# Output weights put into head order on the chip, attention outputs multiplied with them directly, and finer loads near the end: a decode attention kernel on Trainium2

## Chip, cores and metric

The kernel runs on one core of one Trainium2 chip. The metric is the device time of one execution in microseconds (us): before the change a median of 1379.54 us over three runs, from 1379.39 to 1380.29. The profile read below is of one execution with a span of 1378.5 us and a mean granted TensorE clock of 0.905.

## What is computed

Two attention blocks for a single decode step. Both have 4 batch rows, 32 query heads of size 128, a model width of 512 and bf16 data. Block A has 8 key/value heads and looks at the last 2048 positions only; block B has 32 key/value heads and looks at all 8192 positions. The two results stand side by side in the output.

```
def _B_ref(x, k_cache, v_cache, wq, wo):
    B, Sq, D = x.shape                      # 4, 1, 512
    H, Dh = 32, 128
    q = (x @ wq).reshape(B, Sq, H, Dh).transpose(0, 2, 1, 3)
    scores = einsum("bhqd,bhkd->bhqk", q, k_cache) * (Dh ** -0.5)
    p = softmax(scores)
    o = einsum("bhqk,bhkd->bhqd", p, v_cache)
    return o.transpose(0, 2, 1, 3).reshape(B, Sq, H * Dh) @ wo
# A: the same with 8 key/value heads, each used by 4 query heads,
#    and only the last 2048 of 8192 positions
```

B's keys and values are 268 MB each, out of 587.51 MB that the whole kernel moves.

## The kernel before

**Chunks.** Block A is 8 chunks (one per key/value head, all four batch rows). Block B is 32 chunks: one chunk is four heads of one batch row. They are taken group by group: a group is four heads (`hq`, 0 to 7), and inside a group the four batch rows follow one another. A chunk of B is 256 tiles of 128 x 128 keys and as many of values, 8.39 MB each.

**The work on one chunk of B** (`whole_B`, L771) is written out in program order for every engine:

1. 32 steps `g`, each of 8 tiles: TensorE transposes the 8 key tiles into a PSUM bank of `tr` (`emit_T`, three banks), VectorE or ScalarE copies them to `kt` in SBUF, and two steps later TensorE multiplies them with the query `qq` into the scores `sc` (`emit_S`).
2. Statistics: VectorE takes the row maxima (`stats_rowmax`), TensorE turns them (`stats_gmax`), VectorE reduces, TensorE spreads the result (`stats_bc`), VectorE writes `negb`.
3. ScalarE takes the exponentials in eight instructions, two halves of four heads (`exp_B`), VectorE sums them (`sums_B`).
4. 256 matmuls of probabilities with value tiles into `po` (`emit_pv`); at step 20 of 32 the sums are turned into reciprocals (`norm_sum`).
5. `norm_out` scales `po` into `oz`, a 128 x 16 tile that holds four heads of this batch row and zeros elsewhere.

**Output projection.** The weights of a group, `wos`, are loaded as they lie in HBM: partition p holds rows 4p to 4p+3 of the group's 512 rows. So a head's 128 rows lie on 32 partitions, four rows on each, while `oz` has a head's 128 values on 128 partitions. Before the change the outputs are brought into the order of the weights: `emit_sel` (L679) multiplies `oz` with four 0/1 matrices `sel4` into `ms`, and four small copies put the result into `zB`. Then `emit_fin` (L700) adds to `fin` with 8 matmuls, four for each half of the 512 output columns. For chunk c-1 these two stand inside the keys of chunk c: `emit_sel` after step g = 1, `emit_fin` after g = 4. For the last chunk they stand after everything else, and `emit_out` copies `fin` to SBUF and starts the stores.

**Loads and their order.** All loads of keys, values and weights are issued in one fixed order by one queue, SyncE's, and a load that waits holds up all those behind it. Keys have one buffer of a chunk's size, values have one. The keys of chunk c+1 come in two pieces of 128 tiles; a piece may start when the chunk c has transposed the quarters of the buffer that it overwrites. The values of chunk c+1 are one piece and may start when all 256 value matmuls of chunk c are done. Exceptions at the end: the last chunk's keys come in pieces of `LASTK`, its values in `LASTV`, the values of the last but one in `NEXTV` = (128, 64, 64) tiles. GpSimd waits for each piece and counts it into the semaphores `r_k` and `r_v`, which TensorE waits on before certain steps (`QK`, `QV`).

For the first chunk of each group but the first, the queue holds: two key pieces, then `wos` of the new group, then the values. The reload of `wos` waits for `emit_fin` of the last chunk of the old group (L344), which is in step 4 of the chunk just begun.

Of the kernel before, what the change touches and what calls it, by code (L numbers as in the profile page):

```python
# [6 lines left out]
ACTF = mybir.ActivationFunctionType  # L7
# [160 lines left out]
def bass_concat_heads__sliding_block_cached__mha_block_cached__decode_kernel(  # L168
# [39 lines left out]
    NTA, NTB = chunks[0]["NT"], chunks[-1]["NT"]  # L208
    NONE = NC
    chunks.append(dict(chunks[NCA]))  # L210
    assert sum(LASTV) == sum(LASTK) == sum(NEXTV) == NTB and NTA * 16 == 1024 and NTB * 4 == 1024

    sch = _Sched()
    with ExitStack() as es:
        block = es.enter_context(nc.Block())

        def sb(name, shape, dt):
            return es.enter_context(nc.sbuf_tensor(name, shape, dt))
# [47 lines left out]
        semnames += [f + str(i) for f, x in (("d_lk", LASTK), ("d_lv", LASTV), ("d_nv", NEXTV)) for i in range(len(x))]  # L266
# [31 lines left out]
        for r in range(4):  # L298
            sch.add("pool", lambda e, r=r: e.affine_select(
                out=sel4[:, r, :], in_=onesb[:, :], pattern=[[0, 4], [-4, 32]], compare_op=ALU.is_equal,  # L300
                fill=0.0, base=-r, channel_multiplier=1), waits=["c_onesb"], key="c_sel" if r == 3 else None)


        half_of = {}
# [34 lines left out]
        def dma_wos(hq):  # L339


            src = B_wo[4 * hq * P:4 * (hq + 1) * P, :].rearrange("(p r) n -> p (r n)", r=4)
            sch.add_dma("sp", lambda e: e.dma_start(wos[:, :, :].rearrange("p r n -> p (r n)"), src), "d_wos",
                        waits=[("fin", NCA + 4 * hq - 1)] if hq else [], key=("wos", hq))  # L344

        def dma_A(kind, c):
            ch = chunks[c]
# [6 lines left out]
        def dma_B(kind, c):  # L354


            ch = chunks[c]
            T, at, steps = (B_k, KB, QK) if kind == "k" else (B_v, VB, QV)
            src = T[ch["b"], 4 * ch["hq"]:4 * ch["hq"] + 4].rearrange("u (pp j) d -> (u pp) (j d)", pp=P // 4)
            dst = flat(at, 4)  # L360
            if kind == "k":
                pieces, fam = (LASTK, "d_lk") if c == NC - 1 else ((NTB // 2,) * 2, "d_bk")
            else:
                pieces, fam = (LASTV, "d_lv") if c == NC - 1 else (NEXTV, "d_nv") if c == NC - 2 else ((NTB,), "d_bv")
            j0, unit = 0, NTB // 4
            for i, n in enumerate(pieces):
                waits = []
                for u in range(j0 // unit, (j0 + n - 1) // unit + 1):
                    waits += held[at + u]
                x = slice(j0 * P, (j0 + n) * P)  # L370
                sch.add_dma("sp", lambda e, x=x: e.dma_start(dst[:, x], src[:, x]), fam + str(i), waits=waits, key=(kind, c, i))
                j0 += n
                sch.relay("pool", sems, "r_" + kind, n // TG, [(kind, c, i)] + ([("wos", ch["hq"])] if i == 0 and (kind == "v" if c > NCA else kind == "k") else []))
# [292 lines left out]
        def norm_out(c):  # L666
            if c < NCA:
                m = c % NSM
                o, i0, i1 = oT[:, m, :], po[:, m * 16:m * 16 + 16], rinv[:, m, :]
                waits = [("rinv", c), ("pv", c)] + ([("sm", c - 2)] if c >= 2 else [])  # L670
            else:

                o, i0 = oz[:, :].rearrange("p (b u) -> p b u", b=NB), bcast(po[:, 0:4], [[0, NB], [1, 4]])
                i1 = rz[:, :].rearrange("p (b u) -> p b u", b=NB)
                waits = [("rz", c), ("pv", c), ("sm", prev(c))]
            sch.add("dve", lambda e: e.tensor_tensor(out=o, in0=i0, in1=i1, op=ALU.mult), waits=waits, key=("oT", c))  # L676
            po_read[:] = [("oT", c)]

        def emit_sel(c):  # L679

            ab = 0 if c < NCA else 1
            if ab == 0:
                x, z, free = oT[:, c % NSM, :], zA[:, c % 2, :], [("fin", c - 2)] if c >= 2 else []
            else:
                x, z, free = oz[:, :], zB[:, :], [("fin", prev(c))] if c != NONE else []
            for r in range(4):
                pe_mm(ms[:, Z0 + r * 16:Z0 + (r + 1) * 16], sel4[:, r, :], x,
                      waits=([("oT", c)] if c != NONE else []) + (["c_oz", "c_sel"] if ab else []) + ms_read if r == 0 else [], key=("sm", c) if r == 3 else None)
            for h in range(4):
                pp = slice(h * P // 4, (h + 1) * P // 4)  # L690
                src, dst = ms[pp, Z0:Z0 + 64].rearrange("p (r b h) -> p h r b", r=4, b=NB)[:, h], z[pp, :].rearrange("p (r b) -> p r b", r=4)
                if c == NC - 1 and h % 2:
                    sch.add("act", lambda e, src=src, dst=dst: e.activation(dst, src, ACTF.Copy),
                            waits=[("sm", c)] + free if h == 1 else [], key=("z2", c) if h == 3 else None)
                else:
                    sch.add("dve", lambda e, src=src, dst=dst: e.tensor_copy(dst, src),  # L696
                            waits=[("sm", c)] + free if h == 0 else [], key=("z", c) if h == (2 if c == NC - 1 else 3) else None)
            ms_read[:] = [("z", c)] + ([("z2", c)] if c == NC - 1 else [])

        def emit_fin(c):  # L700
            ab = 0 if c < NCA else 1
            if ab == 1:
                ops = [(zB[:, r * NB:(r + 1) * NB], wos[:, r, :]) for r in range(4)]
                waits = [("z", c)] + ([("z2", c)] if c == NC - 1 else [])
# [12 lines left out]
            if c == lastc:  # L717
                emit_out(c)
# [52 lines left out]
        def whole_B(c):  # L771


            ch, p = chunks[c], prev(c)
            sch.mark()
            emit_qb(c)
            for g in range(ch["NG"]):
                emit_T(ch["s"] + g)
                if g == 1:
                    emit_sel(p)  # L780
                if g == 4:
                    emit_fin(p)
                if g >= SLAG:
                    emit_S(ch["s"] + g - SLAG)
                if g == ch["NG"] // 2 + SLAG + 1:
                    stats_rowmax(c, 0)
            for g in range(SLAG):
                emit_S(ch["s_last"] + 1 - SLAG + g)
            stats_rowmax(c, 1)
            stats_gmax(c)  # L790
            stats_bc(c)
            exp_B(c)
            sums_B(c)
            for g in range(ch["NG"]):
                emit_pv(c, g)
                if g == 20:
                    norm_sum(c)
            norm_out(c)
# [86 lines left out]
```

## Time and profile before

| | before |
|---|---|
| device time, median of 3 | 1379.54 us (1379.39 to 1380.29) |
| span of the profiled execution | 1378.5 us |
| bytes moved, mean rate | 587.51 MB, 426 GB/s |
| TensorE matmul busy | 1161.0 us (84%) |
| VectorE busy | 682.3 us (49%) |
| ScalarE busy | 514.0 us (37%) |
| chain of waits: DMA | 54% |
| chain of waits: TensorE | 40% |
| largest link: landing of B's values | 47% |

The busy shares of engines are averages over stages in which different things end last, so they only say where to look. The strip of 40 slices shows at what time an engine or the DMA was busy. The chain of waits follows the last instruction back to what released it, step by step; an entry such as "DMA kv<-in_B_v_cache_dram" is the time from the issue of a load to its landing, in which other loads ahead of it in the queue are included.

### The profile page before, as it was taken

What the parts mean: (1) busy time and instruction counts of PE and PEld (TensorE: products, weight loads), DVE (VectorE), ACT (ScalarE), POOL (GpSimd) and SP (SyncE); (2) the same over time, 40 slices, a digit from 0 to 9 for tenths busy, and PEclk for the clock granted to TensorE, in tenths of its full rate; (3) what the DMA queues carried; (4) which work ended last, traced back from release to release, by engine and by line L of the source; (5) the groups of instructions that cost most, each with busy time, mean ns of one, the idle gap of its engine ahead of it and who ended that gap; (6) DMA issues with size and microseconds to landing.
All of it is one profiled execution on the core that took longest, in us unless ns stands there. A gap on an engine that the chain in (4) does not pass through costs nothing.

```text
span 1378.5 us, 60077 instructions
## 1 busy us (share of the span) xinstructions
PE 1161.0 (84%) x27036; PEld 1117.0 (81%) x27037; DVE 682.3 (49%) x1337; ACT 514.0 (37%) x651; POOL 6.8 (0%) x24
## 2 busy tenths in 40 slices
PE   4898788889888788898888788898888888988887
PEld 4786688889887788888888788898878788987887
DVE  1675355555444445554444455554444455544444
ACT  1553234433333334433333344333333344333333
POOL 1000000000000000000000000000000000000000
PEclk9998899999999989999999898998999999989999
DMA  9999999999999999999999999999999999999996
GB/s 401 425 426 442 415 425 432 433 422 443 430 434 434 426 433 433 434 438 435 430 430 424 434 435 431 434 440 434 432 428 430 431 434 433 441 430 432 428 421 260
DMA packets 20220, 587.51 MB, mean 426 GB/s; under 512 B 2260, under 2 KB 2280, under 8 KB 4712
## 3 DMA queue, kind: packets, MB, share of 16 engines
q1 hardware_dynamic: 20168, 587.21, 99.1%
q8 instruction: 15, 0.25, 0.1%
q14 instruction: 5, 0.04, 0.0%
q10 hardware_dynamic: 32, 0.01, 0.0%
HBM read 587.21 MB, written 0.01 MB: 426 GB/s over the span
## 4 chain that ended last, share of the span: by engine, by line
DMA 54%; PE 40%; DVE 3%; issue 2%; ACT 1%; SPq 0%; DVEq 0%; POOLq 0%; ACTq 0%
DMA kv<-in_B_v_cache_dram 47%; PE po L407 22%; PE tr L405 10%; DMA kv<-in_B_k_cache_dram 6%; PE sc L407 6%; DMA kv<-in_B_wq_dram 2%; PE ms L407 1%; ACT pbb L587 1%; PE fin L407 1%; DVE kt L472 1%; DVE sA L525 1%; DVE rh L541 0%; PE ms L405 0%; DVE rm L537 0%; DVE sA L523 0%
## 5 line engine op out<-in xcount | busy, mean ns | idle before, releaser
L405 PE MATMUL tr<-identb,kv 128*128 128x128 bf16 x8704 | 660.6, 220 | 9.7 <-POOLq L71 4.9
L470 ACT ACTIVATE kt<-tr 128x1024 bf16<-128x1024 bf16 x352 | 359.6, 1024 | 720.2 <-PE tr L405 720.0
L472 DVE COPY kt<-tr 128x1024 bf16<-128x1024 bf16 x736 | 499.2, 690 | 209.1 <-PE tr L405 205.4
L405 PEld LDWEIGHTS tr<-identb,kv 128*128 128x128 bf16 x8704 | 505.9, 98 | 15.2 <-issue 5.7
L407 PE MATMUL po<-pbb,kv 128*128 128x64 bf16 x8192 | 311.9, 208 | 118.2 <-POOLq L71 97.9
L407 PE MATMUL sc<-qq,kt 128*128 128x64 bf16 x8192 | 397.9, 191 | 15.3 <-DVE kt L472 11.2
L407 PEld LDWEIGHTS po<-pbb,kv 128*128 128x128 bf16 x8192 | 308.4, 109 | 120.4 <-issue 63.2
L407 PEld LDWEIGHTS sc<-qq,kt 128*128 128x128 bf16 x8192 | 328.1, 98 | 27.8 <-DVE kt L472 14.3
L587 ACT ACTIVATE pbb<-sc,negb 32x128 bf16<-32x128 f32 x256 | 137.3, 536 | 124.2 <-DVE negb L570 121.0
L592 DVE TENSOR_REDUCE rsb<-pbb 128x4 f32<-128x1024 bf16 x32 | 39.0, 1220 | 142.7 <-ACT pbb L587 142.7
L654 DVE RECIPROCAL rinv<-ms 128x4 f32<-128x4 f32 (+1 forms) x40 | 7.8, 196 | 162.1 <-PE ms L407 162.1
L541 DVE TENSOR_REDUCE rh<-sc 128x4 f32<-128x512 f32 x64 | 43.9, 686 | 14.3 <-PE sc L407 14.3
L405 PE MATMUL ms<-identf,rm 128*4 128x128 f32 x40 | 11.1, 276 | 35.2 <-DVE rm L544 31.4
L676 DVE TENSOR_TENSOR oz<-po,rz 128x16 bf16<-128x16 f32 x32 | 5.6, 175 | 67.4 <-PE po L407 67.4
L405 PEld LDWEIGHTS ms<-identf,rm 128*4 128x4 f32 x40 | 3.2, 81 | 39.3 <-DVE rm L544 34.3
L407 PE MATMUL sc<-qb,kt 128*128 128x64 bf16 (+3 forms) x512 | 26.0, 196 | 0.5 <-issue 0.2
L407 PEld LDWEIGHTS ms<-gm,ind 4*128 4x128 f32 x64 | 10.5, 203 | 18.1 <-DVE gm L556 18.1
L407 PE MATMUL po<-pba,kv 128*128 128x64 bf16 x512 | 20.5, 199 | 3.7 <-issue 2.3
L407 PEld LDWEIGHTS sc<-qb,kt 128*128 128x128 bf16 x512 | 21.8, 101 | 2.0 <-issue 1.4
L407 PE MATMUL ms<-gm,ind 4*128 4x4 f32 x64 | 13.3, 276 | 11.9 <-DVE gm L556 11.9
L696 DVE CAST zB<-ms 32x16 bf16<-32x16 f32 x130 | 21.8, 168 | 1.7 <-PE ms L407 0.4
L407 PEld LDWEIGHTS po<-pba,kv 128*128 128x128 bf16 x512 | 17.9, 102 | 5.7 <-ACT pba L609 4.2
(61 smaller groups left out, 207.1 us busy)
## 6 DMA issues: line engine op xcount, KB each, us to landing
kv<-in_B_k_cache_dram SPq DMA_DIRECT2D x62, 4096.0 KB, 26.7
kv<-in_A_k_cache_dram SPq DMA_DIRECT2D x8, 2048.0 KB, 12.4
kv<-in_A_v_cache_dram SPq DMA_DIRECT2D x8, 2048.0 KB, 13.8
kv<-in_B_v_cache_dram SPq DMA_DIRECT2D x2, 4096.0 KB, 19.3
kv<-in_B_v_cache_dram SPq DMA_DIRECT2D x3, 2048.0 KB, 24.5
kv<-in_B_k_cache_dram SPq DMA_DIRECT2D x3, 2048.0 KB, 26.5
kv<-in_A_wq_dram SPq DMA_DIRECT2D x1, 4096.0 KB, 12.2
kv<-in_B_wq_dram SPq DMA_DIRECT2D x1, 4096.0 KB, 27.1
```

The lines of the kernel that those rows point to most:

```text
L405: sch.add("pe", lambda e: e.transpose(o, l, r), waits, key)
L407: sch.add("pe", lambda e: e.matmul(o, l, r, start=start, stop=stop), waits, key)
L470: sch.add("act", lambda e: e.activation(dst, src, ACTF.Copy), waits=waits, key=("ev", s))
L472: sch.add("dve", lambda e: e.tensor_copy(dst, src), waits=waits, key=("ev", s))
L525: emit = lambda e, src=src, b=b: e.scalar_tensor_tensor(out=t, in0=src, scalar=mk[:, b:b + 1], in1=t, op0=ALU.mult, op1=ALU.add)
L541: sch.add("dve", lambda e: e.tensor_reduce(out=rh[:, half, :], in_=src, axis=AX.X, op=ALU.max), waits=[("S", ch["s"] + (half + 1) * ch["NG ...
L587: sch.add("act", lambda e, src=src, dst=dst, pp=pp, u=u: e.activation(dst, src, ACTF.Exp, bias=negb[pp, 0, u:u + 1], scale=scale), waits=[ ...
L592: sch.add("dve", lambda e: e.tensor_reduce(out=rst[1][:, :], in_=probs_of(c).rearrange("p j u -> p u j"), axis=AX.X, op=ALU.add), waits=[( ...
L654: sch.add("dve", lambda e: e.reciprocal(out=ri, in_=ms[:, L0:L0 + n]), waits=[("L", c)], key=("rinv", c))
L676: sch.add("dve", lambda e: e.tensor_tensor(out=o, in0=i0, in1=i1, op=ALU.mult), waits=waits, key=("oT", c))
L696: sch.add("dve", lambda e, src=src, dst=dst: e.tensor_copy(dst, src), waits=[("sm", c)] + free if h == 0 else [], key=("z", c) if h == (2 ...
```

## The change

The weights are brought into head order instead of the outputs. In each chunk of B, after the last scores, 16 matmuls (`reorder`) multiply the 32 partitions of `wos` that hold one head u with 0/1 matrices `back`, four per head, and leave that head's 128 x 512 weights in a bank of `tr`. Four copies by VectorE (`take_wol`) put them into `wol`, which lies in a part of `kv` that block B doesn't use. `emit_fin` then takes `oz` as it is, together with `wol`; `emit_sel`, its copies and `zB` go away for block B, and `emit_fin` moves from step 4 to step 1 of the following chunk. Three heads are reordered ahead of the turn of the maxima, the fourth after it, since there are three banks.

Since `wos` is now read by `reorder` and not by `emit_fin`, its reload waits for the last reordering of the old group, and it has been put ahead of the new group's keys in the queue. The purpose is a shorter end after the last values and a values load that doesn't wait for the projection. Besides, the keys of the last chunk but one come in three pieces (`NEXTK`), and the values of the last chunk but two in the three pieces of `NEXTV`.

```
+NEXTK = (64, 64, 128)
...
-        zB = sb("zB", [P, 16], BF16)
+        back = sb("back", [P, 4, P], BF16)
+        wol = kv[:, 8, 0:4 * DO].rearrange("p (u n) -> p u n", u=4)
...
             sch.add_dma("sp", lambda e: e.dma_start(wos[:, :, :].rearrange("p r n -> p (r n)"), src), "d_wos",
-                        waits=[("fin", NCA + 4 * hq - 1)] if hq else [], key=("wos", hq))
+                        waits=[("reord", NCA + 4 * hq - 1)] if hq else [], key=("wos", hq))
...
-                pieces, fam = (LASTK, "d_lk") if c == NC - 1 else ((NTB // 2,) * 2, "d_bk")
+                pieces, fam = (LASTK, "d_lk") if c == NC - 1 else (NEXTK, "d_nk") if c == NC - 2 else ((NTB // 2,) * 2, "d_bk")
             else:
-                pieces, fam = (LASTV, "d_lv") if c == NC - 1 else (NEXTV, "d_nv") if c == NC - 2 else ((NTB,), "d_bv")
+                pieces, fam = (LASTV, "d_lv") if c == NC - 1 else (NEXTV, "d_nv") if c in (NC - 2, NC - 3) else ((NTB,), "d_bv")
...
         for c in range(NCA, NC):
-            if c == NCA:
-                dma_wos(0)
+            if (c - NCA) % NB == 0:
+                dma_wos((c - NCA) // NB)
             dma_B("k", c)
-            if c > NCA and (c - NCA) % NB == 0:
-                dma_wos((c - NCA) // NB)
             dma_B("v", c)
...
+        def reorder(c, u, bank):
+            pp = slice(u * P // 4, (u + 1) * P // 4)
+            o = tr[:, bank, :].bitcast(F32)
+            for r in range(4):
+                pe_mm(o, back[pp, r, :], wos[pp, r, :], start=r == 0, stop=r == 3,
+                      waits=([("wol", c, 0)] if u == 3 else [("c_back", 3)]) if r == 0 else [], ...)
+
+        def take_wol(c, u, bank):
+            o = tr[:, bank, :].bitcast(F32)
+            sch.add("dve", lambda e: e.tensor_copy(wol[:, u, :], o), ...)
...
-                ops = [(zB[:, r * NB:(r + 1) * NB], wos[:, r, :]) for r in range(4)]
+                ov = oz[:, :].rearrange("p (b u) -> p b u", b=NB)
+                ops = [(ov[:, :, u], wol[:, u, :]) for u in range(4)]
...
                 emit_T(ch["s"] + g)
                 if g == 1:
-                    emit_sel(p)
-                if g == 4:
                     emit_fin(p)
...
             stats_rowmax(c, 1)
+            reorder(c, 0, 0)
+            reorder(c, 1, 1)
+            reorder(c, 2, 2)
             stats_gmax(c)
             stats_bc(c)
             exp_B(c)
+            for u in range(3):
+                take_wol(c, u, u)
+            reorder(c, 3, 0)
+            take_wol(c, 3, 0)
             sums_B(c)
...
         sch.mark()
-        emit_sel(NC - 1)
         emit_fin(NC - 1)
```

More of the change, by code (lines that the diff above doesn't have):

```diff
@@ L210, in bass_concat_heads__sliding_block_cached__mha_block_cached__decode_kernel @@
     chunks.append(dict(chunks[NCA]))
-    assert sum(LASTV) == sum(LASTK) == sum(NEXTV) == NTB and NTA * 16 == 1024 and NTB * 4 == 1024
+    assert sum(LASTV) == sum(LASTK) == sum(NEXTK) == sum(NEXTV) == NTB and NTA * 16 == 1024 and NTB * 4 == 1024
     sch = _Sched()
@@ L265, in bass_concat_heads__sliding_block_cached__mha_block_cached__decode_kernel @@
         semnames += ["d_h%d" % i for i in range(NH)] + ["d_bk0", "d_bk1", "d_bv0"]
-        semnames += [f + str(i) for f, x in (("d_lk", LASTK), ("d_lv", LASTV), ("d_nv", NEXTV)) for i in range(len(x))]
+        semnames += [f + str(i) for f, x in (("d_lk", LASTK), ("d_nk", NEXTK), ("d_lv", LASTV), ("d_nv", NEXTV)) for i in range(len(x))]
         semnames += ["d_wo%d" % i for i in range(NWO)] + ["d_wos"]
@@ L301, in bass_concat_heads__sliding_block_cached__mha_block_cached__decode_kernel @@
                 fill=0.0, base=-r, channel_multiplier=1), waits=["c_onesb"], key="c_sel" if r == 3 else None)
+        sch.add("pool", lambda e: e.memset(back[:, :, :], 0.0), waits=["c_sel"], key="c_back0")
+        for u in range(4):
+            sch.add("pool", lambda e, u=u: e.affine_select(
+                out=back[:, :, :], in_=back[:, :, :], pattern=[[1, 4], [-1, P]], compare_op=ALU.not_equal,
+                fill=1.0, base=-P * u, channel_multiplier=4), waits=["c_back0" if u == 0 else ("c_back", u - 1)], key=("c_back", u))
         half_of = {}
@@ L372, in dma_B @@
                 j0 += n
-                sch.relay("pool", sems, "r_" + kind, n // TG, [(kind, c, i)] + ([("wos", ch["hq"])] if i == 0 and (kind == "v" if c > NCA else kind == "k") else []))
+                sch.relay("pool", sems, "r_" + kind, n // TG, [(kind, c, i)] + ([("wos", ch["hq"])] if i == 0 and kind == "k" and ch["b"] == 0 else []))
             for g, end in zip(steps, steps[1:] + (NTB // TG,)):
@@ L674, in norm_out @@
                 i1 = rz[:, :].rearrange("p (b u) -> p b u", b=NB)
-                waits = [("rz", c), ("pv", c), ("sm", prev(c))]
+                waits = [("rz", c), ("pv", c), ("fin", prev(c))]
             sch.add("dve", lambda e: e.tensor_tensor(out=o, in0=i0, in1=i1, op=ALU.mult), waits=waits, key=("oT", c))
@@ L679, in emit_sel @@
         def emit_sel(c):
[L681 to L685, printed above, removed]
+            z = zA[:, c % 2, :]
             for r in range(4):
-                pe_mm(ms[:, Z0 + r * 16:Z0 + (r + 1) * 16], sel4[:, r, :], x,
-                      waits=([("oT", c)] if c != NONE else []) + (["c_oz", "c_sel"] if ab else []) + ms_read if r == 0 else [], key=("sm", c) if r == 3 else None)
+                pe_mm(ms[:, Z0 + r * 16:Z0 + (r + 1) * 16], sel4[:, r, :], oT[:, c % NSM, :],
+                      waits=[("oT", c)] + ms_read if r == 0 else [], key=("sm", c) if r == 3 else None)
             for h in range(4):
@@ L691, in emit_sel @@
                 src, dst = ms[pp, Z0:Z0 + 64].rearrange("p (r b h) -> p h r b", r=4, b=NB)[:, h], z[pp, :].rearrange("p (r b) -> p r b", r=4)
[L692 to L698, printed above, removed]
+                sch.add("dve", lambda e, src=src, dst=dst: e.tensor_copy(dst, src),
+                        waits=[("sm", c)] + ([("fin", c - 2)] if c >= 2 else []) if h == 0 else [], key=("z", c) if h == 3 else None)
+            ms_read[:] = [("z", c)]
+        def reorder(c, u, bank):
[3 more added lines that the diff above has]
+                pe_mm(o, back[pp, r, :], wos[pp, r, :], start=r == 0, stop=r == 3,
+                      waits=([("wol", c, 0)] if u == 3 else [("c_back", 3)]) if r == 0 else [], key=("reord", c) if u == r == 3 else ("reord", c, u) if r == 3 else None)
+        def take_wol(c, u, bank):
+            o = tr[:, bank, :].bitcast(F32)
+            sch.add("dve", lambda e: e.tensor_copy(wol[:, u, :], o),
+                    waits=[("reord", c) if u == 3 else ("reord", c, u)] + [("fin", prev(c))], key=("wol", c, u))
         def emit_fin(c):
@@ L702, in emit_fin @@
             if ab == 1:
-                ops = [(zB[:, r * NB:(r + 1) * NB], wos[:, r, :]) for r in range(4)]
-                waits = [("z", c)] + ([("z2", c)] if c == NC - 1 else [])
+                ov = oz[:, :].rearrange("p (b u) -> p b u", b=NB)
+                ops = [(ov[:, :, u], wol[:, u, :]) for u in range(4)]
+                waits = ["c_oz"] + ([("oT", c), ("wol", c, 3)] if c != NONE else [])
             else:
```

## The prediction

> **What bounds the kernel now.** I read the strip of 40 slices, then the chain of waits, then the issue queue, then single chunks in order of time.
>
> ```profile
> DMA  9999999999999999999999999999999999999996
> GB/s 401 425 426 442 415 425 432 433 422 443 430 434 434 426 433 433 434 438 435 430 430 424 434 435 431 434 440 434 432 428 430 431 434 433 441 430 432 428 421 260
> DMA kv<-in_B_v_cache_dram 47%; PE po L407 22%; PE tr L405 10%; DMA kv<-in_B_k_cache_dram 6%; PE sc L407 6%; DMA kv<-in_B_wq_dram 2%; PE ms L407 1%; ACT pbb L587 1%; PE fin L407 1%; DVE kt L472 1%; DVE sA L525 1%; DVE rh L541 0%; PE ms L405 0%; DVE rm L537 0%; DVE sA L523 0%
> ```
>
> The transfers run at full rate from start to near the end. Values land at 740.34 and, eight chunks later, at 1053.18 (issue plus time to landing in the chain): 39.1 us a chunk for 16.78 MB and a quarter of a weight load (0.13 MB), 432 GB/s. So half a chunk's keys cost 9.7 us, its values 19.4. Up to some 1366 us any gap in the transfers is lost one for one, and TensorE time is free while TensorE waits for values. The last slice is different: no transfers, only work.
>
> The issue queue, columns start, duration, what:
>
> ```profile
> 711.96 0.33 SPq L371 DMA_DIRECT2D kv<-in_B_v_cache_dram  x1
> 723.26 11.15 SPq L371 DMA_DIRECT2D kv<-in_B_k_cache_dram  x2
> 753.90 0.33 SPq L343 DMA_DIRECT2D wos<-in_B_wo_dram  x1
> 754.27 0.44 SPq L371 DMA_DIRECT2D kv<-in_B_v_cache_dram  x1
> ```
>
> This is the last chunk of a group. Its values are issued at 711.96; the two key pieces of the next chunk at 723.26 and about 734 lie behind them, so when the values have landed the engines have 19.4 us of keys to go on with. The reload of wos comes 3.7 us after the value buffer is free (750.2), and by then about 6 us of keys are still queued (9.7 + 9.7 us from 740.3 lasts to 760): that wait costs nothing now.
>
> TensorE in the same chunk (duration, engine, op, in brackets the idle time before it):
>
> ```profile
> 734.84 0.35 PE L407 MATMUL sc<-qq,kt 128*128 128x32 bf16 x8 [0.30 <-DVE kt L472]
> 736.17 0.27 PE L405 MATMUL ms<-identf,rm 128*4 128x128 f32 x1 [0.98 <-DVE rm L544]
> 736.82 0.38 PE L407 MATMUL ms<-gm,ind 4*128 4x4 f32 x2 [0.37 <-DVE gm L556]
> 740.52 2.72 PE L407 MATMUL po<-pbb,kv 128*128 128x64 bf16 x48 [3.32 <-POOLq L71]
> ```
>
> The scores end at 735.19, the values land 5.15 us later. At the other group ends the same distance is 4.9 to 5.8 us. In the last chunk nothing is waited for but work:
>
> ```profile
> 1360.00:1364.00 4.00, 0.65 (x3) 0.37 (x3) 1.29 (x4) 1.74 (x4) 0.00 (x0) 0.79 0.97 396
> 1364.00:1368.00 4.00, 3.55 (x67) 3.55 (x68) 1.22 (x1) 2.55 (x5) 0.00 (x0) 0.50 0.31 116
> 1368.00:1372.00 4.00, 4.00 (x118) 4.00 (x116) 0.13 (x1) 0.00 (x0) 0.00 (x0) 0.86 0.00 0
> 1372.00:1376.00 4.00, 3.19 (x95) 2.75 (x91) 0.74 (x5) 0.35 (x2) 0.00 (x0) 1.00 0.00 0
> ```
>
> Columns: busy PE, PEld, DVE, ACT, POOL, then granted clock, DMA share, GB/s. After the idle stretch the value matmuls run at clock 0.50.
>
> **What the Trainium skill says.** "TensorE: Matmul & The Clock Gate", Part 1 (the HAM clock gate): after an idle window of about 3.4 us the clock is halved until some 3.4 us of work. The trace agrees (0.50 above): 88 value matmuls late in a chunk take 2.60 us (29.5 ns each), the first 168 take 7.18, where 168 x 29.5 ns is 4.96; 2.2 to 2.5 us are lost in each chunk. Same part, on the issue gap: 215.7 ns per warm 512-column matmul; the trace has 0.95 us for block A's four, 238 ns. Part 3 (row/col tiling): matmuls on different 32-row strips overlap; the trace shows the like for column strips only, 8 matmuls of 256 columns in 0.53 us. "DMA: Bandwidth & Descriptors", Queues, rings and completion order: each DMA engine takes its ring in order. The trace agrees: values seen at 427.5, the key half behind them at 437.23, 9.7 us later, though it was issued at 409.90.
>
> **The change, part by part.**
>
> *Reordering, heads 0 to 2.* 12 matmuls go ahead of the turn of the maxima, in program order. Between 2.16 us (a head's four serial, neighbouring heads overlapping by one: 10 x 0.216) and 2.86 us (12 x 0.238). TensorE waited 0.98 us there anyway, so the statistics come 1.2 to 1.9 us later; I take 1.5. The exponentials' first half, 4.45 us after the scores before, comes 5.9 after.
>
> *Copies and head 3.* Turn to negb takes 1.22 us (736.17 to 737.39). Behind it on VectorE stands take_wol of head 0: 0.69 us (block A's 512-column copy from PSUM: 683 ns). Head 3 needs its bank: four matmuls, 0.86 to 0.95. The other copies (2 us) lie under the exponentials, for which VectorE idled 4.47 us; free. With hand-overs of 0.15 the last reordering ends 5.1 to 5.9 us after the scores, middle 5.5.
>
> *Warm clock.* The gap is now half filled, so I expect the value matmuls warm: 7.6 us (256 x 29.5 ns) in place of 10.1. In mid-kernel this frees nothing: the next keys land 9.7 us after the values, so transposes start at 9.9 after the landing where they started at 10.2.
>
> *emit_sel and its copies.* 4 matmuls (0.1 us) and about 0.4 us of stalls behind the copies (1336.66 to 1340.61 holds 3.57 us of work) go; keys and scores take 22.8 us instead of 23.3. In the last chunk 0.8 us of path goes (oz done 1374.6, fin 1375.49).
>
> *The reload of wos.* It waits for head 3 of the group's last chunk, and **all keys of the next group queue behind it**. They were issued while the values were in flight; now nothing is behind the values. Values land 38.8 - 9.9 - 22.8 = 6.1 us after the scores (the same sum with the times of before, 38.8 - 10.25 - 23.3 = 5.25, fits the measured 5.15). The 16 engines don't stop together: at the very end the rate falls from 1364.4 to 1366.2, which puts the mean engine's stop 1.2 us before the landing, at 4.9. The reload is issued at 5.5 and data flow 0.8 us after an issue (first issue 0.81, bytes from about 1.6), at 6.3. Gap 1.4 us, with the bounds above 1.0 to 1.8. Seven reloads; at the first, block B's start has left TensorE behind (scores end 268.2, values due about 269.5); with warm matmuls it catches up most of that, I add 0.7. Sum 7 x 1.4 + 0.7 = **10.5 us lost**. The values' earlier issue gains nothing, as shown.
>
> *The end.* From the landing of the values of chunk NC-3 (1288.45) the kernel took 90.05 us. After: value matmuls 7.6 (their exponentials come about as the values do, so finer pieces there bring nothing); keys of NC-2 22.8, plus 1.1 since their last half lands 19.4 after the values and step 16 comes at 18.5 (the first pieces of NEXTK, landing at 4.9, allow the start at 7.6); statistics 5.9, values 7.6, keys 22.8, statistics 5.9, values 7.6, rest 3.3: 84.6. **Gain 5.4 us.** The finer pieces cost issue time on the queue only, some 0.4 us each, with other loads queued ahead of them: nothing.
>
> GpSimd's five set-up operations run before block B starts: nothing. Sum: 1379.5 + 10.5 - 5.4 = 1384.6, say **1385**.
>
> **The rivals.**
>
> *No gap at the reloads.* If row strips overlap more, or the values land later after the scores than I work out (before: up to 5.8), the reload comes in time and only the end counts: 1379.5 - 5.4 = 1374. For it: a shortfall of 1.4 us is small against the spread of 4.9 to 5.8. Against: it must be won at all seven, and the issue needs 0.8 us ahead of the mean engine's stop.
>
> *Half of it.* Gap 0.7 each: 1379.5 + 5.3 - 5.4 = 1379.4.
>
> *Cold matmuls stay.* The reordering is cut by gaps (turn, reduce, spread, copy); if the clock still halves, value matmuls take 10.1, transposes start 10.5 after the landing, values come 5.5 after the scores, gap 2.0: 14.7 us in all; the end takes 91.4 (0.4 + three times 10.1, twice 22.8 and 5.9, and 3.3), 1.3 more. 1379.5 + 14.7 + 1.3 = 1395.5. Against: the longest pure idle stretch falls to about 1.3 us.
>
> **How the numbers follow.** Forecast as worked out 0.58; no gap 0.20; half 0.10; cold 0.12. Within 0.2% means 1376.8 to 1382.3: the half case and a few of the forecast's low end (0.14 together). Faster: the rival without gap, 0.20. Slower: the rest, 0.66. The range goes from 1374 to 1395.
>
> **What would show it.** The keys of a group's first chunk issued about 5.5 us after the last scores and not during them; a dip of 1 to 2 us of full rate in the transfers at seven places, some 157 us apart; the first transposes of those chunks starting about 12 us after the values' landing and not 10; clock 1.00 in the value matmuls, 7.6 us long; the time from the last transfer to the end about 7 us (84.6 - 77.6) and not 12. If the transfers show no dip, or the value matmuls keep the 0.50, the prediction is wrong in that step.

## The result and the profile after

| | before | after |
|---|---|---|
| device time, median | 1379.49 us (1379.39 to 1380.29, 4 runs) | 1388.88 us (1384.97 to 1389.28, 4 runs) |
| ratio to before | 1 | 1.006, 95% interval 1.0042 to 1.0079 |
| span of the profiled execution | 1378.5 us | 1387.2 us |
| mean granted TensorE clock | 0.905 | 0.918 |
| last bytes arrive at about | 1366.1 us | 1379.5 us |
| from there to the end | 12.4 us | 7.7 us |

The change costs 9.4 us between the medians, and 5.8 to 10.9 us by the interval; the forecast was 5.5. The four runs lie apart by more than 4 us, and the fastest, 1384.97 us, is on the forecast. Ratios here are of mean times of runs in the fast state (within 1.5% of the fastest of their kernel), which leaves out three of the six runs with two buffers below and none elsewhere. The last two rows hold the story: the stream of loads ends 13.4 us later, and the tail behind it is 4.7 us shorter.

The strip of 40 slices and the chain of waits of the kernel after:

```profile
DMA  9999999899999999999999999999999999999997
GB/s 400 425 426 444 413 410 437 364 439 423 440 437 405 426 439 435 427 438 423 440 437 406 435 433 433 444 389 423 454 415 417 435 427 438 423 438 423 423 429 327
DMA kv<-in_B_v_cache_dram 45%; PE po L414 20%; PE tr L412 12%; DMA kv<-in_B_k_cache_dram 8%; PE sc L414 6%; DMA kv<-in_B_wq_dram 2%; PE ms L414 1%; PE tr L414 1%; DMA kv<-in_A_k_cache_dram 1%; PE fin L414 1%; ACT pbb L594 1%; DVE kt L479 1%; DVE sA L532 0%; PE ms L412 0%; DVE gm L563 0%
```

A slice is 34.7 us. The eighth slice (243 to 277 us, the end of block B's first group) has 364 GB/s where it had 433, and slices 13, 22 and 27 (405, 406, 389) hold later group ends. In the chain, landings of keys rise from 6 to 8%: the kernel now waits for keys at places where only values were waited for.

The issue queue at the second group end (start, duration, what):

```profile
432.07 0.33 SPq L352 DMA_DIRECT2D wos<-in_B_wo_dram  x1
432.44 0.91 SPq L380 DMA_DIRECT2D kv<-in_B_k_cache_dram  x2
442.70 0.33 SPq L380 DMA_DIRECT2D kv<-in_B_v_cache_dram  x1
```

Both key pieces go out right behind the reload, 4.8 us after the scores (which end at 427.30). Before, they had been issued while the old values were on the way. What the transfers do meanwhile (columns: stretch, length, busy PE, PEld, DVE, ACT, POOL, granted clock, DMA share, GB/s), at the first and the second group end, and last, to compare, three lines of the kernel before at its second group end, where the scores end at 421.82 and the values land 5.7 us later:

```profile
268.00:272.00 4.00, 3.25 (x57) 2.18 (x54) 2.54 (x6) 0.49 (x1) 0.00 (x0) 1.00 0.12 49
272.00:276.00 4.00, 3.22 (x33) 1.93 (x34) 2.61 (x5) 3.75 (x7) 0.00 (x0) 0.62 0.12 30
...
426.00:430.00 4.00, 2.63 (x42) 1.55 (x39) 2.68 (x7) 0.46 (x1) 0.00 (x0) 1.00 1.06 459
430.00:434.00 4.00, 2.67 (x20) 1.24 (x21) 2.02 (x5) 3.84 (x8) 0.00 (x0) 0.50 0.39 133
434.00:438.00 4.00, 4.00 (x99) 4.00 (x97) 1.19 (x1) 0.00 (x0) 0.00 (x0) 0.65 1.11 457
...
426.00:428.00 2.00, 0.29 (x7) 0.33 (x8) 0.00 (x0) 1.94 (x5) 0.00 (x0) 0.50 0.99 426
428.00:430.00 2.00, 2.00 (x42) 2.00 (x40) 1.22 (x1) 0.51 (x1) 0.00 (x0) 0.50 0.91 393
430.00:432.00 2.00, 2.00 (x65) 2.00 (x63) 0.00 (x0) 0.00 (x0) 0.00 (x0) 0.88 1.10 475
```

From 430 to 434 only 133 GB/s arrive. At the first group end the DMA stands nearly still for 8 us of the record. (The bytes of a packet are booked at its start, and a packet of the values is a 64 KB row that takes 2.4 us, so the true pause is that much shorter than the record shows: no byte moves for about 4.5 us, from 271.0 to 275.5.)

The cost can be added up from when the value matmuls of each group's first chunk start:

| group | 2 | 3 | 4 | 5 | 6 | 7 | 8 | end |
|---|---|---|---|---|---|---|---|---|
| before, us | 311.38 | 467.79 | 624.19 | 780.61 | 937.00 | 1093.43 | 1249.85 | 1378.5 |
| after, us | 316.89 | 474.50 | 631.57 | 790.27 | 947.94 | 1105.66 | 1263.05 | 1387.2 |
| after minus before | 5.51 | 6.71 | 7.38 | 9.66 | 10.94 | 12.23 | 13.20 | 8.7 |

A group took 156.4 us each time; it now takes 157.1 to 158.7. The six later group ends cost 7.7 us, 1.28 each. By the first one 5.5 us are lost. How long the pause is there depends on how late TensorE is, because the reload now hangs on TensorE's work. In this execution TensorE was late: it finished the scores of block B's first chunk at 156.0 us and not at 153.5, after waits of some 2 us that nothing in the trace explains, and the transfers dip from 160 to 180 us (379 GB/s against 424). Such waits are there before too and differ from run to run. A run below with the same order of loads ("The change without the finer pieces") had those scores at 153.4 us and starts the second group's value matmuls only 1.2 us later than the kernel before. The end gives back 4.5 us.

TensorE at the second group end (start, duration, instruction, in brackets the idle time before it), and behind the dots the kernel before at the same place:

```profile
426.95 0.35 PE L414 MATMUL sc<-qq,kt 128*128 128x32 bf16 x8 [0.30 <-DVE kt L479]
427.24 1.06 PE L414 MATMUL tr<-wos,back 32*128 32x512 bf16 x12
428.92 0.38 PE L414 MATMUL ms<-gm,ind 4*128 4x4 f32 x2 [0.37 <-DVE gm L563]
430.16 1.88 PE L414 MATMUL tr<-wos,back 32*128 32x512 bf16 x4 [0.85 <-DVE kv L709]
433.22 6.67 PE L414 MATMUL po<-pbb,kv 128*128 128x64 bf16 x168 [1.17 <-POOLq L72]
439.94 2.73 PE L414 MATMUL po<-pbb,kv 128*128 128x64 bf16 x88
445.47 0.73 PE L412 MATMUL tr<-identb,kv 128*128 128x128 bf16 x10 [2.80 <-POOLq L72]
...
421.47 0.35 PE L407 MATMUL sc<-qq,kt 128*128 128x32 bf16 x8 [0.30 <-DVE kt L472]
427.70 6.30 PE L407 MATMUL po<-pbb,kv 128*128 128x64 bf16 x168 [3.82 <-POOLq L71]
437.40 1.06 PE L405 MATMUL tr<-identb,kv 128*128 128x128 bf16 x16 [0.61 <-POOLq L71]
```

The 12 matmuls of heads 0 to 2 take 1.06 us and fit into the time in which TensorE waited before. The four of head 3 wait for the first copy (0.85 us) and here take 1.88 us, because the clock has just been halved (at 429.96). TensorE was not idle when that happened; in the 3.41 us up to there it was busy for 2.08:

```profile
426.55:429.96 3.41, 2.08 (x27) 1.01 (x23) 2.09 (x6) 0.42 (x1) 0.00 (x0) 1.00 1.20 519
```

The first transposes wait 2.80 us for keys and start 12.3 us after the value matmuls did; before, the distance was 9.7.

The end, to be held against the four lines shown in the prediction (same columns as above):

```profile
1370.00:1374.00 4.00, 2.68 (x20) 0.99 (x19) 3.07 (x8) 1.71 (x4) 0.00 (x0) 1.00 1.03 438
1374.00:1378.00 4.00, 3.51 (x81) 3.52 (x82) 1.85 (x3) 2.60 (x5) 0.00 (x0) 0.68 0.94 387
1378.00:1382.00 4.00, 4.00 (x123) 4.00 (x120) 0.36 (x2) 0.00 (x0) 0.00 (x0) 0.89 0.37 138
```

The value matmuls of the last chunk, after and (behind the dots) before:

```profile
1374.49 6.62 PE L414 MATMUL po<-pbb,kv 128*128 128x64 bf16 x168 [0.58 <-ACT pbb L594]
1381.17 2.73 PE L414 MATMUL po<-pbb,kv 128*128 128x64 bf16 x88
...
1364.45 7.18 PE L407 MATMUL po<-pbb,kv 128*128 128x64 bf16 x168 [2.47 <-ACT pbb L587]
1371.69 2.73 PE L407 MATMUL po<-pbb,kv 128*128 128x64 bf16 x88
```

In its last chunk the kernel before had the clock at 0.50 from 1362.3 to 1369.1, of which 4.7 us lay under value matmuls. Now it is at 0.50 from 1375.4 to 1378.9, 3.4 us of it under value matmuls. The halving comes later and is shorter here; it has not gone, and in mid-kernel (429.96 to 436.79) it lasts 6.8 us as before.

### The profile page after: what moved, and what is told of

Same layout as the page of the kernel before. It is cut to its first block, busy times and chain, and to the rows that moved or that the text cites. A ratio compares the mean times of both kernels' runs of the same rounds, so it can differ in the third digit from the quotient of the medians.

```text
span 1387.2 us, 60816 instructions
## 1 busy us (share of the span) xinstructions
PE 1234.2 (89%) x27417; PEld 1137.9 (82%) x27417; DVE 744.6 (54%) x1335; ACT 513.9 (37%) x649; POOL 9.8 (1%) x29
## 4 chain that ended last, share of the span: by engine, by line
DMA 55%; PE 41%; DVE 2%; issue 1%; ACT 1%; SPq 0%; POOLq 0%; DVEq 0%
DMA kv<-in_B_v_cache_dram 45%; PE po L414 20%; PE tr L412 12%; DMA kv<-in_B_k_cache_dram 8%; PE sc L414 6%; DMA kv<-in_B_wq_dram 2%; PE ms L414 1%; PE tr L414 1%; DMA kv<-in_A_k_cache_dram 1%; PE fin L414 1%; ACT pbb L594 1%; DVE kt L479 1%; DVE sA L532 0%; PE ms L412 0%; DVE gm L563 0%
## 5 line engine op out<-in xcount | busy, mean ns | idle before, releaser
L414 PEld LDWEIGHTS sc<-qq,kt 128*128 128x128 bf16 x8192 | 331.6, 98 | 15.7 <-DVE kt L479 13.1
L414 PE MATMUL tr<-wos,back 32*128 32x512 bf16 x512 | 80.5, 408 | 27.3 <-DVE kv L709 27.3
L661 DVE RECIPROCAL rinv<-ms 128x4 f32<-128x4 f32 (+1 forms) x40 | 7.8, 196 | 158.7 <-PE ms L414 158.7
L709 DVE CAST kv<-tr 128x512 bf16<-128x512 f32 x128 | 81.3, 683 | 12.3 <-PE tr L414 12.3
L414 PEld LDWEIGHTS tr<-wos,back 32*128 32x128 bf16 x512 | 23.2, 96 | 49.1 <-DVE kv L709 30.1
```

What stands on the lines that cost most here:

```text
L414: sch.add("pe", lambda e: e.matmul(o, l, r, start=start, stop=stop), waits, key)
L661: sch.add("dve", lambda e: e.reciprocal(out=ri, in_=ms[:, L0:L0 + n]), waits=[("L", c)], key=("rinv", c))
L709: sch.add("dve", lambda e: e.tensor_copy(wol[:, u, :], o), waits=[("reord", c) if u == 3 else ("reord", c, u)] + [("fin", prev(c))], key=( ...
```

## The experiments

Each ratio is to the kernel before, run on the same chip in the same series; brackets hold the 95% interval. The main theory is that the reload's wait holds up the keys behind it and nothing else slows the kernel.

### Keys ahead of the reload again

The rest of the change stays.

```
-            if (c - NCA) % NB == 0:
-                dma_wos((c - NCA) // NB)
+            if c == NCA:
+                dma_wos(0)
             dma_B("k", c)
+            if c > NCA and (c - NCA) % NB == 0:
+                dma_wos((c - NCA) // NB)
             dma_B("v", c)
# the reload is counted with the group's second piece of keys, not the first
-    [("wos", ch["hq"])] if i == 0 and ...
+    [("wos", ch["hq"])] if i == 1 and ...
```

> The changed kernel with the two key pieces of a group's first chunk issued ahead of the reload of wos again, as before the change (GpSimd's count of the second key piece then waits for the reload too); reordering, direct use and finer pieces stay. Reload theory (the loss is keys held back behind the reload's wait): no gap in the transfers at the seven group ends, transfers end at 1366 as before, and the end keeps its gain of 4.7 us: 1374.8 us, 0.3% faster than the kernel before. Work theory (the 16 matmuls and 4 copies of each chunk cost the time): still about 1388. Half and half: near 1381.

Measured: 1377.05 us, ratio 0.9978 (0.997 to 0.9986). The queue of this kernel at the second group end:

```profile
401.61 0.33 SPq L380 DMA_DIRECT2D kv<-in_B_v_cache_dram  x1
412.49 11.15 SPq L380 DMA_DIRECT2D kv<-in_B_k_cache_dram  x2
428.92 0.33 SPq L352 DMA_DIRECT2D wos<-in_B_wo_dram  x1
```

The keys are under way from 412 on, the reload at 428.92 holds up nothing that is needed, the rate from 430 to 434 is 475 GB/s, and the groups are again 156.4 us apart (626.77, 783.20, 939.59, 1095.98, 1252.37). So moving the reload behind the keys turns the loss into a small gain, with all the reordering in place: the reordering isn't what costs. The gain is smaller than the 1374.8 us that was expected. In the profiled execution the end takes 125.83 us from the last group's value start, 2.8 less than before and not 4.5 less; the clock is again at 0.50 for 6.8 us, from 1362.9 to 1369.7, though the reordering is the same as in the change, and the value matmuls of each of the last three chunks take 10.0 us instead of the change's 9.4. Why the halving was shorter in the end of the change's one profiled execution is not shown.

### The same, with the gaps of TensorE filled

On top of the experiment above: seven extra matmuls of 512 columns in each chunk, on constants, into `po` before it is used. Their results aren't used.

```
+        def fill(n):
+            for i in range(n):
+                pe_mm(po[:, :], identb[:, :], sel4[:, :, :].rearrange("p r n -> p (r n)"), ...)
...
             stats_bc(c)
+            fill(4)
             exp_B(c)
...
             reorder(c, 3, 0)
+            fill(3)
```

> As the run with the keys first, and seven matmuls of 512 columns on constants into po, which nothing reads, added per chunk: four ahead of the reordering of head 3, three after it, to fill TensorE's idle time between the scores and the value matmuls. Clock theory (the clock is halved for idle time in this gap): clock 1.00 through the value matmuls, 7.6 us each instead of 9.4 in the last chunks, and three such stages in the end give 4 to 5 us: about 1370. Rival (the clock is halved for another reason, or the matmuls on a constant tile don't count): the same time as the run with the keys first, 1374.8, or up to 1 us more where the added matmuls delay the value matmuls.

Measured: 1371.82 us, ratio 0.9946 (0.9933 to 0.9959), the fastest of all kernels here; mean clock 0.971. The last value matmuls on TensorE, and the end by stretches:

```profile
1358.22 0.82 PE L416 MATMUL po<-sel,identb 128*128 128x512 bf16 x3
1358.87 5.06 PE L416 MATMUL po<-pbb,kv 128*128 128x64 bf16 x168
1364.00 2.73 PE L416 MATMUL po<-pbb,kv 128*128 128x64 bf16 x88
```

```profile
1355.00:1359.00 4.00, 3.63 (x25) 1.36 (x20) 3.13 (x8) 2.35 (x5) 0.00 (x0) 1.00 0.99 418
1359.00:1363.00 4.00, 4.00 (x143) 4.00 (x141) 1.23 (x2) 1.99 (x4) 0.00 (x0) 1.00 0.94 380
```

168 value matmuls take 5.06 us at clock 1.00, where they take 6.67 in the kernel after at its second group end. Groups stay 156.4 us apart; from the last group's value start to the end it is 121.2 us (1248.88 to 1370.1), 7.4 less than before and 4.6 less than without the fill. This is the warm case that the prediction had expected of the change itself. Seven matmuls don't fill every gap: where a group's first values come 7.4 us after the scores, at six of seven places, the value matmuls still take 9.3 to 10.5 us. That costs nothing, since the next keys land later anyway.

### The change without the finer pieces

`NEXTK` and the finer values of the last chunk but two are undone:

```
-   (LASTK, "d_lk") if c == NC - 1 else (NEXTK, "d_nk") if c == NC - 2 else ((NTB // 2,) * 2, "d_bk")
+   (LASTK, "d_lk") if c == NC - 1 else ((NTB // 2,) * 2, "d_bk")
...
-   (NEXTV, "d_nv") if c in (NC - 2, NC - 3) else ((NTB,), "d_bv")
+   (NEXTV, "d_nv") if c == NC - 2 else ((NTB,), "d_bv")
```

> The changed kernel with only the finer pieces undone: keys of the last chunk but one in two pieces, values of the last chunk but two in one. Reload theory: the losses at the group ends stay; the end is longer by the wait of the value matmuls of chunk NC-3 for the whole values (1.6 us) and of the next transposes for half the keys, less a wait of 0.9 at their second half: about 1 us in all, 1389 to 1390. Rival (the finer pieces themselves slow the transfers): 1 us or more faster than the changed kernel, below 1388.

Measured: 1386.87 us, ratio 1.0053 (1.0035 to 1.007). The interval lies for the most part on that of the change itself (1.0042 to 1.0079), and the expected 1389 to 1390 us did not come: no effect that can be told from the times. The trace shows why. In this execution TensorE was not late in the first group, and the second group's value matmuls start at 312.57 us, 4.3 ahead of the change's; the six later group ends cost 1.13 us each; and the end is longer, 127.75 us from the last group's value start where the change has 124.2. The first difference, which varies from run to run, hides the last.

### The kernel before with the finer pieces alone

The same lines, the other way round, in the kernel before.

> The kernel before with only the finer pieces added (NEXTK for the last chunk but one, NEXTV also for the last but two). The value matmuls of chunk NC-3 started at 1288.60 with the landing of all values, the exponentials were ready 1.4 us earlier; the next transposes started at 1298.93 and can start up to 1.4 earlier with the first 64 key tiles. I expect a gain of 1 to 1.4 us: 1378.2. Rival (the pieces cost something in the transfers): 1379.5 or more.

Measured: 1378.24 us, ratio 0.9991 (0.9979 to 1.0004). The interval holds both the expected gain and none. Inconclusive as a time. Its trace shows where a gain can come from: the value matmuls of the last chunk but two start 4.7 us after the scores, before the last of their values have landed, where they started 6.0 after.

### Two buffers for the reloaded weights

In the kernel after, two buffers in turn, so that the reload waits for a group that was done long ago:

```
+        wos2 = [wos[:, :, :], kv[:, 9, 0:4 * DO].rearrange("p (r n) -> p r n", r=4)]
...
-    waits=[("reord", NCA + 4 * hq - 1)] if hq else [], key=("wos", hq))
+    waits=[("reord", NCA + 4 * (hq - 1) - 1)] if hq > 1 else [], key=("wos", hq))
...
-    pe_mm(o, back[pp, r, :], wos[pp, r, :], ...)
+    pe_mm(o, back[pp, r, :], wos2[hq % 2][pp, r, :], ...)
```

> The changed kernel with its order of loads (reload of wos ahead of the keys), but with two buffers for wos used in turn by the groups, so that the reload waits for a reordering one group earlier, long done. It tells the order of the loads from the wait. If the wait does it (reload theory as written): no gap at the group ends, values 156.4 us apart per group as before, 1377 us as with the keys first (0.998 of the kernel before). If the mere place of the reload ahead of the keys does it: 157.7 per group, near 1388.

Measured: 1485.31 us over all six runs (1463.01 to 1497.52), ratio 1.0655 (1.0603 to 1.0707). It tells nothing of the theories. The addresses now alternate between groups, and the code folds chunks into a loop only where their instructions have the same addresses, so TensorE's program is no longer the same loop. The queue that fetches instructions (packets, MB, share of 16 engines):

```profile
q8 instruction: 114, 1.87, 0.5%
```

It is 15 packets and 0.25 MB in all the other kernels. The wait list of TensorE in the profiled execution (1497.52 us, the slowest of the six) is led by idle time without a releaser (us in total, times, longest):

```profile
PE tr L413 <- issue: 70.8, 26, 6.4
```

That the fetches cause these stretches is likely, and was not shown.

### The same idea with every engine's program kept

The reload stays ahead of the keys, but goes into a buffer of its own, and GpSimd copies it to `wos` once the old group has been reordered:

```
+        stage = kv[:, 9, 0:4 * DO]
...
-    e.dma_start(wos[:, :, :]..., src)   # waits for ("reord", NCA + 4 * hq - 1)
+    e.dma_start(stage, src)             # waits for ("wcopy", hq - 1)
...
+    sch.add("pool", lambda e: e.tensor_copy(wos[:, :, :]..., stage),
+            waits=[("wos", hq)] + ([("reord", NCA + 4 * hq - 1)] if hq else []), key=("wcopy", hq))
# and GpSimd counts the group's second piece of keys after this copy
```

> The changed kernel with its order of loads (reload of wos ahead of the keys), but the reload goes into a buffer of its own and waits for nothing recent; GpSimd copies it to wos once the group's last reordering is done, seven times in mid-kernel, and counts the second key piece after that. TensorE's, VectorE's and ScalarE's programs stay as they are, in their loops. The wait as cause: the keys are issued while the values are in flight, 156.4 us per group, and the time is that of the keys-first kernel, ratio 0.998, about 1377. The place in the queue as cause: 157.7 per group and a ratio of 1.006.

Measured: 1377.56 us, ratio 0.998 (0.9973 to 0.9987). The queue of this kernel:

```profile
398.38 0.33 SPq L381 DMA_DIRECT2D kv<-in_B_v_cache_dram  x1
398.75 0.43 SPq L353 DMA_DIRECT2D kv<-in_B_wo_dram  x1
409.26 11.15 SPq L381 DMA_DIRECT2D kv<-in_B_k_cache_dram  x2
```

The reload is in the same place in the queue as in the change, ahead of the keys, and is issued at once; the groups are 156.4 us apart. So it is the wait of the reload that costs, not its place.

### The reload made to wait longer

In the kernel after, the reload waits for the last value matmul of the old group instead of its last reordering:

```
-    waits=[("reord", NCA + 4 * hq - 1)] if hq else [], key=("wos", hq))
+    waits=[("pv", NCA + 4 * hq - 1)] if hq else [], key=("wos", hq))
```

> The changed kernel with the reload of wos waiting for the last value matmul of the group's last chunk instead of the last reordering. A larger dose of the suspected wait: the reload is issued 10.2 us after the values land and not about 1 us before it. The transfers stand still from the landing to 0.8 us after the issue at seven group ends, 11 us each against the 1.3 of the changed kernel. Reload theory: 1388.9 + 7 x 9.7 = 1457 us, the values of a group's first chunk 12 us later than 157.7 after the group before, so about 167.5 per group. Work theory: no more than a few us over 1389.

Measured, in a single run: 1464.89 us. First group end of this kernel, by stretches:

```profile
270.00:274.00 4.00, 3.74 (x41) 2.35 (x42) 2.09 (x4) 3.90 (x8) 0.00 (x0) 0.50 0.00 0
274.00:278.00 4.00, 4.00 (x98) 4.00 (x96) 1.22 (x1) 0.04 (x1) 0.00 (x0) 0.65 0.00 0
278.00:282.00 4.00, 4.00 (x135) 3.95 (x131) 0.36 (x2) 0.00 (x0) 0.00 (x0) 1.00 0.00 0
```

No transfer starts in these 12 us; the reload goes out at 282.11. The groups are 167.7 to 170 us apart: a longer wait of this one load costs about what it is longer, at every group end.

### The kernel before, filled

In the kernel before, without any of the change: 4 and 10 extra matmuls of the same kind.

```
+            fill(4)
             stats_gmax(c)
             stats_bc(c)
+            fill(10)
             exp_B(c)
```

> The kernel before with nothing of the change, and 14 matmuls of 512 columns on constants into po per chunk, four ahead of the turn of the maxima and ten between the spread and the value matmuls, as filling. It tells what warm value matmuls are worth without reordering. Clock theory: clock 1.00 in the value matmuls, 7.6 us where 10.1 were; in mid-kernel nothing, in the end two or three stages of 2.4 us: 1379.5 - 6 = about 1373.5 (ratio 0.9955), some 1.5 us behind the filled kernel with the keys first, which has no emit_sel in the end and finer pieces. Rival (what made the filled kernel fast was reordering and direct use): 1379 or more.

Measured: 1374.59 us, ratio 0.996 (0.9945 to 0.9976), clock 0.979. With the finer pieces added to it:

> The kernel before with the filling matmuls and the finer pieces, without reordering and direct use. What it lacks of the filled keys-first kernel (1371.8, ratio 0.9946) is the change's own end without emit_sel (0.8 us): I expect 1372.8, ratio 0.9952. If reordering and direct use are worth more than that, it stays at the 1374.6 of the filled kernel before.

Measured: 1372.86 us, ratio 0.9951 (0.9938 to 0.9964). The five runs lie between 1372.72 and 1373.16, the six without the finer pieces between 1374.01 and 1377.10. The ratios' intervals overlap, but with the clock kept up the finer pieces seem to be worth some 1.5 us. The best version, with the reordering and the fill, has 0.9946. These intervals overlap too, and about 1 us is left that direct use of the outputs can be worth once the clock is kept up. The larger part of the best version's gain is the clock's.

### The change with its order of loads, filled

The seven extra matmuls, and the reload ahead of the keys as in the change.

> The changed kernel with its order and its wait, and the seven filling matmuls. The clock decides whether the reordering of head 3 takes 1.0 or 1.9 us, and with it how late the reload is. Clock as a part of the loss: reload issued 3.9 to 4.1 us after the scores at all seven group ends, no late start at the first; loss per group from 1.3 down to about 0.5 us, 3.5 in all, and the end as in the filled keys-first kernel (1371.8): 1375.5. If the gap doesn't depend on the clock: 1371.8 + 7 x 1.3 and more at the first group's end, 1382 to 1384.

Measured: 1381.81 us, ratio 1.0014 (1.0001 to 1.0027). With the clock kept up, the reload goes out 4.0 us after the scores at all seven group ends, 0.7 to 0.8 earlier than at the first two of the change, and the first group's loss shrinks (from the value matmuls of its last chunk to those of the next 40.2 us, against 42.4 after the change and 37.5 with the keys ahead). It is some 6 to 7 us better than the change, but each later group still loses about 1.6 us (value starts 156.7 to 159.4 apart, 158.0 in the mean), so the clock is not why the gap is there. A part of it can be seen on TensorE:

```profile
440.92 1.88 PE L412 MATMUL tr<-identb,kv 128*128 128x128 bf16 x16 [4.96 <-POOLq L72]
```

The keys land late and TensorE is idle for 4.96 us; the clock is then at 0.50, so the first 16 transposes take 1.88 us (in the kernel with the keys ahead 1.06), and two more sets of eight 1.03 us each instead of 0.61. That this accounts for all of the 1.6 us wasn't shown.

## Why the prediction was partly right

**The cause: right.** The keys queue behind the reload's wait. The order of loads alone (0.9978), the same place without the wait (0.998), and the longer wait (1464.89 us) say so together.

**Size of a later group end: right in size, 1.28 us each where 1.4 were forecast, but in part by luck.** Two terms in its sum were off and partly cancelled. The values land 5.2 to 6.0 us after the scores (forecast 6.1). The reload goes out 3.9 to 4.8 us after the scores (forecast 5.5). By the prediction's own sum the gap should then have been 0 to 1.3 us, 0.7 in the mean. A part of the rest can be seen at the second group end: bytes flow only 0.9 us after the issue, and then the sixteen engines start unevenly (172, 369, 401 GB/s in the first three half microseconds, against 432). That this makes up the whole difference at every group end was not shown. The rival without a gap had named what came true, strips that overlap more; the gap stayed all the same.

**The first group end: wrong in size, 5.5 us where 2.1 were forecast.** This is the term that mis-sized the total. The prediction let TensorE catch up with warm matmuls by then. They stayed cold, and in this execution TensorE had started block B late: the scores end at 269.92, 1.5 us ahead of the values' landing (it was 2.8 before; the prediction reckoned with 1.3 there and with a catch-up). So of the 4.65 us to the reload and the 0.9 to the first bytes, the prediction's own sum leaves some 5.2 bare. The filled version of the change, in which TensorE is faster, loses less there, as this reading asks. Some 2 us of the 5.5 are the late start, which varies: the kernel with the keys first, which started as late (156.4), is 2.3 us behind at the second group, and the one without the finer pieces, which did not, is 1.2 us behind in spite of the wait.

**Reordering of heads 0 to 2: wrong.** It was costed at 2.16 to 2.86 us and a delay of the statistics of 1.5. It took 1.06 us and delayed nothing: the value matmuls can start 4.47 us after the scores, as before (1374.49 less 1370.02, and 1364.45 less 1359.98). The prediction let only neighbouring heads overlap by one matmul; 12 matmuls on three row strips take as long as four on one (1.03). "TensorE: Matmul & The Clock Gate", Part 3 of the Trainium skill, says that different row strips overlap; the trace agrees, and more fully than the prediction read it.

**Warm clock: wrong.** The value matmuls of the last chunk take 9.35 us and not 7.6; in mid-kernel they take 9.0 to 10.5. The step that failed is the argument against the rival of cold matmuls, that no pure idle stretch over 1.3 us would be left: the clock was halved at 429.96 though TensorE had been busy for 2.08 of the 3.41 us before and had not been idle for more than 0.7 us at a time. A rule of an idle window, as the prediction cites it, doesn't fit this; the measurement decides. Half filling the gap didn't do; filling it did. The rival was thus right on the clock, but its sum was not, as it kept the 1.5 us of delayed statistics.

**The end: 4.5 us gained, 5.4 forecast, near by luck.** Two stages of statistics were put 1.4 us too long each and two of value matmuls 1.8 too short, which nearly cancels. The first of the three value stages is as cold, but starts 1.5 us earlier after the scores than before, because the finer pieces let it begin ahead of the last values. The tail behind the last transfer is 7.7 us (forecast about 7).

**Finer pieces: nothing was forecast, and the times can't tell; in the traces they matter.** With the statistics put 1.5 us too late, the prediction had the exponentials ready only about when all values had landed. They were ready earlier, so the pieces had something to give:

```profile
1300.16 6.62 PE L414 MATMUL po<-pbb,kv 128*128 128x64 bf16 x168 [0.58 <-ACT pbb L594]
...
1288.60 7.51 PE L407 MATMUL po<-pbb,kv 128*128 128x64 bf16 x168 [3.99 <-POOLq L71]
```

In the last chunk but two, these value matmuls start after a wait of 0.58 us for the exponentials, where before they waited 3.99 us for the values.

The sum on the measured terms: 5.5 + 7.7 - 4.5 = 8.7 us of span, of which the change isn't shown to cause the some 2 us of the late start.

## What to carry to other kernels

In a queue that issues in order, a load that waits holds up every load behind it, also those that could go at once. Put it behind the loads that it doesn't concern, or give it a buffer so that it needn't wait, and ask of each place in the queue how many microseconds of transfers are still under way when the wait begins. When a matmul stage follows a gap on the path, read its granted clock, and don't take short work in the gap for enough; a few matmuls without use in the gap were worth more here (5 to 7 us) than the whole change of the projection. A load that waits for an engine's work is also as late as that engine, and that can vary from run to run. When an experiment alternates buffers, look at the instruction transfers before its time is read.

## What was not expected of the hardware

- 12 matmuls of 32 x 512 on three row strips, written strip after strip, took 1.06 us, and the four of one strip 1.03. In the trace they start in threes; the three that end a head's sum start within 0.03 us of one another (427.89 to 427.92).
- The clock was halved while TensorE was far from idle: 2.08 us of work in the last 3.41. Two bursts of such matmuls of about 1 us each in the gap of some 4.5 us didn't keep the clock up; seven full-size ones of 512 columns more did (0.50 against 1.00 in the value matmuls).
- With addresses that alternate between groups, 1.87 MB of instructions were transferred instead of 0.25, and even the fastest run took 1463.01 us; that the one causes the other was not shown.
